# Sliding-window attention with a gated MLP: q loaded by 16 tokens per partition and turned straight through

## The chip, the cores and the metric

The kernel runs on one core of a Trainium2 chip. Its time is the device time of one launch in microseconds (us). The engines are named as in the profile: PE (TensorE, with PEld for its weight loads), DVE (VectorE), ACT (ScalarE), POOL (GpSimd) and SP (SyncE), which here only issues transfers. Sixteen DMA engines move the data between HBM and the on-chip memory SBUF.

## The reference

Eight batches, eight heads, 576 tokens, head size 64. Attention is causal in a window of 64 tokens; its output, with the heads side by side, goes through a gated MLP whose gate mixes the tokens with a 576 x 576 matrix.

```python
scores = scale * np.matmul(q, k.transpose(0, 1, 3, 2))     # scale = 1/8
mask = (rel >= 0) & (rel < 64)                             # rel = query token - key token
attn = softmax(np.where(mask, scores, -1e9))
x = matmul(attn, v), heads side by side                    # [8, 576, 512]
h = np.maximum(x @ w_in, 0.0);  u, v = h[..., :512], h[..., 512:]
v_n = (v - mean(v)) / sqrt(var(v) + 1e-6)
v_s = einsum('ts,bsd->btd', w_spatial, v_n) + b_spatial[None, :, None]
out = (u * v_s) @ w_out                                    # [8, 576, 512], float32
```

## The kernel before

The work is cut into named steps, and a table `ORDER` fixes by hand the order in which each engine's steps are issued, with the engine of the steps that may run on several. A step is named by its kind, its batch, and its part: `S4_1` are the score products of batch 4, head group 1. Engines run their steps in this order and wait for each other through semaphores. The SP queue (DQ in the table) issues all loads and nearly all stores, also in order; a store or a load whose buffer is not free holds up what is queued behind it.

A head group is four heads. For each batch and group, `load_steps` makes these steps for q, and the same for k:

- `ldq`: one transfer of the group's q, 4 heads x 576 tokens x 64 float32, into the tile `nq` of 128 partitions. Partition 32h + i holds 18 tokens in a row of head h, 18i to 18i + 17, a run of 4608 bytes.
- `cq`: a cast to float16, into `hq`, on POOL (three pieces), ACT or DVE as the table says.
- `tq`: one DVE transpose. Two float16 are taken as one float32, so a token is 32 such pairs. The instruction turns each 32 x 32 block by itself. Block j holds token 18i + j of all i, and it is written with a step of 18 pairs (72 bytes), so that in `qT` a partition holds one pair of head-size positions of one head, and the tokens stand in their order.

In `att_steps`, the step `S` computes the scores on PE. Each head has 32 partitions, and a product handles 64 keys and 64, 128 or 192 queries of one head. Each pair is two float16, so there are two products per block (w = 0 and 1), which read every second float16 of kT and qT, 4 bytes from token to token. A step has 64 products, into two PSUM pairs. There are 16 such steps, and in `rem_steps` a step `S_r` per batch with 32 products for the last 64 queries. ACT takes the exponentials (`E`, L477), DVE the mask (`M`, L480), PE the sums and the products with v (`Z`, `P`), ACT the inverse (`N`, `n`) and DVE the scaling (`X`, L512). The MLP follows with `V` and `U` (products with w_in), `A` (normalized), `G` (mixing over tokens) and `O` (w_out), its evacuations `Vr`, `Ur` and `Oe` on ACT and `Ge` on DVE, and the stores `st`. PE alternates between the attention of one batch and the MLP of the batches before it. Twenty-five steps `D` on zeros keep PE going in the first stage.

Tiles come from rings of buffers: eight for `nq`, `nk` and the weights' staging together, four for the cast `hq`/`hk`, six for `qT`/`kT`. v is loaded in pieces of 128 tokens, in runs of 256 bytes.

Of the kernel before, what the change touches and what calls it, by code (L numbers as in the profile page):

```python
# [169 lines left out]
class Plan:  # L170
# [3 lines left out]
    def add(self, name, engs, key, fn, deps=(), acq=(), uses=(), mode=None, nbytes=0, n=0):  # L174
        if isinstance(engs, tuple):
            engs = [engs]
        s = Step(name, engs, key, fn, deps, acq, uses, mode, nbytes, n)
        s.n = len(self.steps)
        self.steps.append(s)
        return s  # L180
# [17 lines left out]
def kernel(  # L198
# [11 lines left out]
    nc = tc.nc  # L210
    f16 = dt.float16
    f32 = dt.float32
# [67 lines left out]
    def buf(tag, name):  # L280
        b = Buf(tag, name)
        if tag in SHAPES:
            shape, d = SHAPES[tag]
            b.make = lambda i: pool.tile(shape, d, tag=f"{tag}_{i}", bufs=1, name=name)
        return b

    plan = Plan()
    add = plan.add
    ENG = {"ACT": nc.scalar, "DVE": nc.vector, "POOL": nc.gpsimd, "PE": nc.tensor, "DQ": nc.sync}

    def cp(e, o, i):
        if e == "ACT":
            nc.scalar.copy(o, i)  # L293
        elif e == "POOL" and len(i.shape) == 2 and i.shape[1] > 1000:
            for n in (0, 384, 768):
                nc.gpsimd.tensor_copy(o[:, n:n + 384], i[:, n:n + 384])  # L296
        elif e == "POOL" and len(i.shape) == 4 and i.shape[1] > 2:
            for lo, hi in ((0, 2), (2, i.shape[1])):
                nc.gpsimd.tensor_copy(o[:, lo:hi, :, :], i[:, lo:hi, :, :])
        else:  # L300
            ENG[e].tensor_copy(o, i)

    def cost(n, a=True, d=True, p=True, d1=False):

        out = []
        if a:
            out.append(("ACT", 0.09 + 0.00083 * n))
        if d:
            out.append(("DVE", 0.07 + (0.00104 if d1 else 0.00053) * n))
        if p:  # L310
            out.append(("POOL", 0.14 + 0.00083 * n))
        return out
# [81 lines left out]
    KT, QT, HV, HS, DKT, DQT, DHV, XB, XD = {}, {}, {}, {}, {}, {}, {}, {}, {}  # L394

    def load_steps(b, g, key):
        early = b < 2

        def one(name, src, key):
            n = buf("nat", f"n{name}{b}_{g}")  # L400
            ld = add(f"ld{name}{b}_{g}", ("DQ", 0.45), key, lambda e: nc.sync.dma_start(
                n.t[:, :], src[b, 4 * g:4 * g + 4, :, :].rearrange("h (i j) d -> (h i) (j d)", j=18)),
                acq=[n], nbytes=1.57, n=128)
            h = buf("hqk", f"h{name}{b}_{g}")
            c = add(f"c{name}{b}_{g}", cost(1152, d=early), key,
                    lambda e: cp(e, h.t[:, :], n.t[:, :]), deps=[ld], acq=[h], uses=[n])
            qt = buf("qkT", f"{name}T{b}_{g}")
            d = add(f"t{name}{b}_{g}", ("DVE", 1.09), key, lambda e: nc.vector.transpose(  # L408
                qt.t[:, :].rearrange("p (i j) -> p j i", j=18),
                h.t[:, :].bitcast(f32).rearrange("p (j w) -> p j w", w=32)),  # L410
                deps=[c], acq=[qt], uses=[h])
            return qt, d

        KT[b, g], DKT[b, g] = one("k", k, key)
        QT[b, g], DQT[b, g] = one("q", q, key + 0.001)
        nv = buf("natv", f"nv{b}_{g}")
        lds = []
        for c in range(5):
            sn = 128 if c < 4 else 64
            lds.append(add(f"ldv{b}_{g}{c}", ("DQ", 0.42),  # L420
                           key + 0.002 + 0.0001 * c,
                           lambda e, c=c, sn=sn: nc.sync.dma_start(  # L422
                               nv.t[0:sn, c, :, :],
                               v[b, 4 * g:4 * g + 4, 128 * c:128 * c + sn, :].transpose([1, 0, 2])),
                           deps=lds[-1:], acq=[] if c else [nv], uses=[nv] if c else [],
                           nbytes=0.0051 * sn, n=4 * sn))
        hv = buf("hv", f"hv{b}_{g}")
        hs = buf("hs", f"hs{b}_{g}")
        parts = [(0, 2), (2, 4)] if early else [(0, 4)]
        done = []  # L430
        for n, (lo, hi) in enumerate(parts):
            w = hi - lo
            l0 = max(lo, 1)
            c = add(f"cv{b}_{g}{n}", cost(256 * w, d=early), key + 0.003,
                    lambda e, lo=lo, hi=hi: cp(e, hv.t[:, lo:hi, :, :], nv.t[:, lo:hi, :, :]),
                    deps=[lds[hi - 1]] + done[:1], acq=[hv] if n == 0 else [],
                    uses=[nv] + ([hv] if n else []))
            sl = add(f"sl{b}_{g}{n}", cost(256 * (hi - l0), d=early), key + 0.0035,
                     lambda e, l0=l0, hi=hi: cp(e, hs.t[0:64, l0:hi, :, :], hv.t[0:64, l0:hi, :, :]),
                     deps=[c] + done[1:2], acq=[hs] if n == 0 else [],  # L440
                     uses=[hv] + ([hs] if n else []))
            su = add(f"su{b}_{g}{n}", cost(256 * w, d=early), key + 0.0035,
                     lambda e, lo=lo, hi=hi: cp(e, hs.t[64:128, lo + 1:hi + 1, :, :],
                                                hv.t[64:128, lo:hi, :, :]),
                     deps=[c, sl if n == 0 else done[1]], uses=[hv, hs])
            done += [c, sl, su]
        done.append(add(f"s4{b}_{g}", cost(256, d=early), key + 0.004, lambda e: cp(
            e, hs.t[0:64, 4, :, :], nv.t[0:64, 4, :, :]), deps=[lds[4], done[1]], uses=[nv, hs]))
        HV[b, g], HS[b, g] = hv, hs
        DHV[b, g] = done  # L450

    def pair16(t):
        return t[:, :].bitcast(f16).rearrange("p (t w) -> p t w", w=2)

    def att_steps(b, g, key):
        sc = [buf("pair", f"sc{b}_{g}{u}") for u in (0, 1)]
        e2 = [buf("e2", f"e2_{b}_{g}{u}") for u in (0, 1)]

        def emit_S(e):
            kT, qT = pair16(KT[b, g].t), pair16(QT[b, g].t)  # L460
            with nc.named_scope(f"S{b}_{g}"):
                for m in range(4):
                    for w in (0, 1):
                        for kap in (2 * m, 2 * m + 1):
                            r = 64 * (kap % 2)
                            c0 = 0 if kap == 1 else 64 * kap
                            c1 = min(512, 64 * kap + 128)
                            for hh in range(4):
                                d = slice(32 * hh, 32 * hh + 32)
                                nc.tensor.matmul(sc[hh // 2].t[r:r + 64, hh % 2, c0:c1],  # L470
                                                 kT[d, 64 * kap:64 * kap + 64, w], qT[d, c0:c1, w],
                                                 start=(w == 0), stop=(w == 1))
        s = add(f"S{b}_{g}", ("PE", 0.6), key, emit_S, deps=[DKT[b, g], DQT[b, g]],
                acq=sc, uses=[KT[b, g], QT[b, g]], mode="s")
# [11 lines left out]
        for u in (0, 1):  # L486
# [3 lines left out]
            def emit_Z(e, u=u, zb=zb):  # L490
                with nc.named_scope(f"Z{b}_{g}{u}"):
# [4 lines left out]
                    acq=[zb], uses=[e2[u]], mode="v")  # L496
            lzd = inverse_steps(f"{b}_{g}{u}", zb, lz, z, key + 0.03 + 0.02 * u, 512)

            def emit_P(e, u=u, ob=ob):
                with nc.named_scope(f"P{b}_{g}{u}"):  # L500
# [7 lines left out]
            p = add(f"P{b}_{g}{u}", ("PE", 0.24), key + 0.04 + 0.02 * u, emit_P,  # L508
                    deps=[mins[u]] + DHV[b, g], acq=[ob], uses=[e2[u], hv, hs], mode="v")
# [17 lines left out]
    def rem_steps(b, key):  # L527
        sc = [buf("pair", f"scr{b}_{u}") for u in (0, 1)]

        def emit_S(e):  # L530
            with nc.named_scope(f"S{b}_r"):
                for g in (0, 1):
                    kT, qT = pair16(KT[b, g].t), pair16(QT[b, g].t)
                    for w in (0, 1):
                        for kap in (8, 7):
                            r = 64 * (kap % 2)
                            for hh in range(4):
                                d = slice(32 * hh, 32 * hh + 32)
                                nc.tensor.matmul(
                                    sc[hh // 2].t[r:r + 64, hh % 2, 64 * g:64 * g + 64],  # L540
                                    kT[d, 64 * kap:64 * kap + 64, w], qT[d, 512:576, w],
                                    start=(w == 0), stop=(w == 1))
        e2 = buf("er", f"er_{b}")
        s = add(f"S{b}_r", ("PE", 0.16), key, emit_S,
# [25 lines left out]
        def emit_P(e):  # L570
            with nc.named_scope(f"P{b}_r"):
# [9 lines left out]
        p = add(f"P{b}_r", ("PE", 0.14), key + 0.04, emit_P, deps=[mn] + DHV[b, 0] + DHV[b, 1],  # L581
                acq=[ob], uses=[e2, HS[b, 0], HS[b, 1]], mode="v")
# [213 lines left out]
    for b in range(B):  # L796
        for g in (0, 1):
            load_steps(b, g, (-1.0 + 0.1 * g) if b == 0 else b - 1.5 + 0.4 * g)
            att_steps(b, g, b + 0.36 * g)
        rem_steps(b, b + 0.72)  # L800
        gmlp_steps(b, b + 1.0)
# [40 lines left out]
```

## Time and profile before

| what | value |
|---|---|
| time, median of 3 runs | 203.01 us (202.39 to 203.58) |
| span of the profiled execution, first to last instruction | 201.0 us |
| mean granted PE clock | 0.996 |
| PE / DVE / ACT / POOL busy | 94% / 80% / 83% / 38% |
| share of DMA engine time in packets of the SP queue | 70.1% |
| DVE transposes of q, of k (16 each) | 1243 ns, 1247 ns |
| loads of q, of k (16 each), issue to landing | 6.4 us, 5.5 us |
| score steps S0_0 and S7_1 begin at | 8.67 us, 158.35 us |

No separate time of the profiled execution is given beside its span; the median of the runs is 2.0 us above the span. In the profile, DMA is the mean busy share of the sixteen DMA engines. Packets are the single runs that a DMA engine moves. In the groups of instructions, a line gives busy time and the mean of one instruction, then the idle time of the engine just before them and who ended it.

### The profile page before, as it was taken

What the parts mean: (1) busy time and instruction counts of PE and PEld (TensorE: products, weight loads), DVE (VectorE), ACT (ScalarE), POOL (GpSimd) and SP (SyncE); (2) the same over time, 40 slices, a digit from 0 to 9 for tenths busy, and PEclk for the clock granted to TensorE, in tenths of its full rate; (3) what the DMA queues carried; (4) which work ended last, traced back from release to release, by engine and by line L of the source; (5) the groups of instructions that cost most, each with busy time, mean ns of one, the idle gap of its engine ahead of it and who ended that gap; (6) DMA issues with size and microseconds to landing.
All of it is one profiled execution on the core that took longest, in us unless ns stands there. A gap on an engine that the chain in (4) does not pass through costs nothing.

```text
span 201.0 us, 7008 instructions
## 1 busy us (share of the span) xinstructions
PE 188.6 (94%) x2927; PEld 97.7 (49%) x2927; DVE 161.2 (80%) x307; ACT 167.0 (83%) x307; POOL 76.5 (38%) x144
## 2 busy tenths in 40 slices
PE   7588889899999999989999999999999999999992
PEld 2233535545445445654455545554465455444450
DVE  4699979999998999699699898979957796647430
ACT  2588799878999899897998989999999999457431
POOL 5202575675894398153757999000000000000000
PEclk9999999999999999999999999999999999999998
DMA  6997999899898876999859995897633004200345
GB/s 221 387 276 184 336 378 210 292 372 377 185 274 255 246 221 188 295 243 234 311 118 262 241 316 178 227 284 249 185 111 117 3 5 132 108 0 0 128 145 202
DMA packets 50275, 42.69 MB, mean 212 GB/s; under 512 B 39361, under 2 KB 39489, under 8 KB 50242
## 3 DMA queue, kind: packets, MB, share of 16 engines
q1 hardware_dynamic: 50018, 41.91, 70.1%
q8 instruction: 23, 0.38, 0.8%
q10 hardware_dynamic: 224, 0.33, 0.5%
q14 instruction: 10, 0.08, 0.1%
HBM read 32.79 MB, written 9.44 MB: 210 GB/s over the span
## 4 chain that ended last, share of the span: by engine, by line
PE 70%; DMA 9%; SPq 7%; ACT 5%; DVE 5%; POOL 1%; issue 1%; POOLq 0%
PE bank L738 16%; PE bank L653 12%; PE bank L763 12%; PE bank L708 10%; DMA nk<-in_k_dram 9%; SPq L422 4%; PE pair L470 4%; PE bank L504 3%; PE bank L666 3%; PE bank L493 3%; PE bank L744 2%; SPq L327 2%; ACT e L477 1%; PE bank L713 1%; ACT ob L610 1%
## 5 line engine op out<-in xcount | busy, mean ns | idle before, releaser
L738 PE MATMUL bank<-wspT,vn 128*128 128x512 f16 (+1 forms) x160 | 37.5, 379 | 0.0
L477 ACT ACTIVATE e<-pair 128x1024 f16<-128x1024 f32 x32 | 31.9, 1027 | 2.7 <-PE pair L470 2.5
L752 DVE TENSOR_TENSOR g<-bank,ru 128x512 f16<-128x512 f32 (+1 forms) x40 | 24.8, 632 | 11.0 <-PE bank L738 5.0
L708 PE MATMUL bank<-x,win 128*128 128x512 f16 x128 | 31.6, 379 | 0.0
L763 PE MATMUL bank<-wout,g 128*128 128x512 f16 x128 | 31.3, 379 | 0.0
L653 PE MATMUL bank<-win,x 128*128 128x512 f16 x128 | 30.4, 379 | 0.2 <-DVE x L512 0.2
L721 ACT ACTIVATE ru<-bank 128x512 f32<-128x512 f32 (+1 forms) x40 | 21.4, 562 | 8.4 <-PE bank L708 4.6
L635 DVE BATCH_NORM_STATS2 st<-vs 128x6 f32<-128x512 f16 (+1 forms) x40 | 25.9, 670 | 3.0 <-ACT vs L633 2.8
L512 DVE TENSOR_TENSOR x<-bank,lz 128x512 f16<-128x512 f32 x32 | 21.2, 683 | 5.4 <-PE bank L504 2.6
L633 ACT ACTIVATE vs<-bank 128x512 f16<-128x512 f32 (+1 forms) x40 | 22.9, 597 | 3.1 <-PE bank L653 2.3
L610 ACT COPY ob<-bank 128x512 f32<-128x512 f32 (+1 forms) x39 | 22.6, 588 | 3.3 <-PE bank L763 3.1
L738 PEld LDWEIGHTS <-vn 128*128 128x128 f16 (+1 forms) x160 | 14.9, 97 | 17.7 <-DVE vn L692 0.5
L480 DVE TENSOR_TENSOR e<-e,mask 128x1024 f16<-128x1024 f16 x32 | 22.5, 721 | 1.0 <-ACT e L477 1.0
L408 DVE STREAM_TRANSPOSE qT<-hq 128x576 f32<-128x576 f32 x16 | 19.7, 1243 | 2.5 <-POOL hq L296 2.3
L296 POOL CAST hq<-nq 128x384 f16<-128x384 f32 x33 | 16.5, 536 | 13.1 <-DMA nq<-in_q_dram 12.5
L408 DVE STREAM_TRANSPOSE kT<-hk 128x576 f32<-128x576 f32 x16 | 20.0, 1247 | 1.4 <-ACT hk L293 1.1
L519 ACT ACTIVATE lz<-bank 128x512 f32<-128x512 f32 x32 | 18.6, 603 | 2.1 <-PE bank L493 2.0
L521 ACT ACTIVATE lz<-lz 128x512 f32<-128x512 f32 x32 | 19.6, 631 | 0.1
L653 PEld LDWEIGHTS <-x 128*128 128x128 f16 x128 | 12.0, 97 | 14.3 <-issue 0.6
L708 PEld LDWEIGHTS <-win 128*128 128x128 f16 x128 | 11.9, 98 | 14.4 <-issue 1.3
L763 PEld LDWEIGHTS <-g 128*128 128x128 f16 x128 | 11.8, 98 | 13.4 <-issue 0.5
L692 DVE TENSOR_SCALAR vn<-vs,mv,ln 128x512 f16<-128x512 f16 (+1 forms) x40 | 15.4, 436 | 3.5 <-ACT ln L682 3.3
(85 smaller groups left out, 294.7 us busy)
## 6 DMA issues: line engine op xcount, KB each, us to landing
nq<-in_q_dram SPq DMA_DIRECT2D x16, 576.0 KB, 6.4
nk<-in_k_dram SPq DMA_DIRECT2D x16, 576.0 KB, 5.5
nv<-in_v_dram SPq DMA_DIRECT2D x64, 128.0 KB, 4.9
out_dram<-ob SPq DMA_DIRECT2D x14, 512.0 KB, 4.6
wi<-in_moe_w_in_dram SPq DMA_DIRECT2D x8, 256.0 KB, 5.6
ws<-in_moe_w_spatial_dram SPq DMA_DIRECT2D x4, 288.0 KB, 8.2
nv<-in_v_dram SPq DMA_DIRECT2D x16, 64.0 KB, 3.6
wo<-in_moe_w_out_dram SPq DMA_DIRECT2D x4, 256.0 KB, 7.1
```

Source lines behind the costliest of these rows:

```text
L408: d = add(f"t{name}{b}_{g}", ("DVE", 1.09), key, lambda e: nc.vector.transpose(qt.t[:, :].rearrange("p (i j) -> p j i", j=18), h.t[:, :].b ...
L477: ex = add(f"E{b}_{g}{u}", ("ACT", 0.91), key, lambda e, u=u: nc.scalar.activation(e2[u].t[:, :, :], sc[u].t[:, :, :], AF.Exp, bias=0.0, s ...
L480: mins.append(add(f"M{b}_{g}{u}", ("DVE", 0.65), key, lambda e, u=u: nc.vector.tensor_tensor(e2[u].t[:, :, :], e2[u].t[:, :, :], mask[:, : ...
L610: lambda e: (nc.vector.tensor_copy if last else nc.scalar.copy)(view(), m.t[rows, 0:n]),
L633: rl = add(f"Vr{b}_{j}", ("ACT", 0.49), key, lambda e: nc.scalar.activation(vs.t[0:jn, :], m.t[0:jn, :], AF.Relu), deps=[pv], acq=[vs], us ...
L635: s1 = add(f"Vb{b}_{j}", ("DVE", 0.6), key + 0.02, lambda e: nc.vector.bn_stats(st6.t[0:jn, 0:6], vs.t[0:jn, :]), deps=[rl], acq=[st6], us ...
L653: nc.tensor.matmul(m.t[:, :], xr(b, r)[:, 128 * j:128 * j + 128], w_in_sb[r][:, 512:1024], start=(r == 0), stop=(r == 3))
L708: nc.tensor.matmul(m.t[:, :], w_in_sb[r][:, 128 * i:128 * i + 128], xr(b, r), start=(r == 0), stop=(r == 3))
L721: lambda e, m=m, ru=ru, n=n: nc.scalar.activation(ru.t[:, 0:n], m.t[:, 0:n], AF.Relu), deps=[pu], acq=[ru], uses=[m])))
L738: nc.tensor.matmul(m.t[:, :], w[0:kn, 128 * i:128 * i + 128], wspT[kk][0:kn, 0:512], start=(kk == 0), stop=(kk == 4))
L752: lambda e, m=m, g=g, ru=ru, n=n: nc.vector.tensor_tensor(g.t[:, 0:n], m.t[:, 0:n], ru.t[:, 0:n], ALU.mult),
L763: nc.tensor.matmul(m.t[:, :], G[r][0].t[:, 128 * j:128 * j + 128], w_out_sb[r][:, :], start=(r == 0), stop=(r == 3))
```

## The change

q is loaded in two transfers. The first brings tokens 0 to 511, 16 tokens per partition (runs of 4096 bytes), the second tokens 512 to 575, two per partition (runs of 512 bytes), both into the same tile. k is loaded as before. The DVE transpose of q then writes its blocks straight through: token 16i + j stands in column 32j + i of `qT`, and token 512 + 2i + j in column 512 + 32j + i. The score products get their queries in the order of tokens by reading q's columns with two steps: 16 (or 2) columns that are 32 pairs (128 bytes) apart, and then on by one pair (4 bytes). The queue table, the casts and the rest are the same.

```diff
+            def load(e):
+                if name == "k":
+                    nc.sync.dma_start(n.t[:, :], src[b, 4 * g:4 * g + 4, :, :].rearrange(
+                        "h (i j) d -> (h i) (j d)", j=18))
+                    return
+                for lo, hi, j in ((0, 512, 16), (512, 576, 2)):
+                    nc.sync.dma_start(n.t[:, 2 * lo:2 * hi], src[b, 4 * g:4 * g + 4, lo:hi, :].rearrange(
+                        "h (i j) d -> h i (j d)", j=j))
...
             d = add(f"t{name}{b}_{g}", ("DVE", 1.09), key, lambda e: nc.vector.transpose(
+                qt.t[:, :], h.t[:, :].bitcast(f32)) if name == "q" else nc.vector.transpose(
                 qt.t[:, :].rearrange("p (i j) -> p j i", j=18),
                 h.t[:, :].bitcast(f32).rearrange("p (j w) -> p j w", w=32)),
...
+    def toks(t, d, lo, hi, w):
+        v16 = t[:, :].bitcast(f16).rearrange("p (t w) -> p t w", w=2)
+        if lo < 512:
+            return v16[d, 0:512, w].rearrange("p (j i) -> p i j", i=32)[:, lo // 16:hi // 16, :]
+        return v16[d, 512:576, w].rearrange("p (j i) -> p i j", i=32)
...
-                                                 kT[d, 64 * kap:64 * kap + 64, w], qT[d, c0:c1, w],
+                                                 kT[d, 64 * kap:64 * kap + 64, w], toks(qT, d, c0, c1, w),
...
-                                    kT[d, 64 * kap:64 * kap + 64, w], qT[d, 512:576, w],
+                                    kT[d, 64 * kap:64 * kap + 64, w], toks(qT, d, 512, 576, w),
```

## The prediction

> **What bounds the kernel now.** I read the page's first two parts, then the chain that ended last, then the windows, then the rows of the lines that the diff touches.
>
> ```profile
> span 201.0 us, 7008 instructions
> PE 188.6 (94%) x2927; PEld 97.7 (49%) x2927; DVE 161.2 (80%) x307; ACT 167.0 (83%) x307; POOL 76.5 (38%) x144
> DMA  6997999899898876999859995897633004200345
> GB/s 221 387 276 184 336 378 210 292 372 377 185 274 255 246 221 188 295 243 234 311 118 262 241 316 178 227 284 249 185 111 117 3 5 132 108 0 0 128 145 202
> DMA packets 50275, 42.69 MB, mean 212 GB/s; under 512 B 39361, under 2 KB 39489, under 8 KB 50242
> PE 70%; DMA 9%; SPq 7%; ACT 5%; DVE 5%; POOL 1%; issue 1%; POOLq 0%
> ```
>
> PE is busy for 94% of the span and carries 70% of the chain: this is a PE-bound kernel after its first 40 us. But the second resource is close behind. The windows (DMA share is the mean busy share of the 16 DMA engines, the last two columns are share and GB/s):
>
> ```profile
> 40.00:50.00 10.00, 9.82 (x160) 5.37 (x160) 9.42 (x14) 7.99 (x14) 6.42 (x13) 1.00 1.06 373
> 0.00:147.00 147.00, 138.61 (x2317) 71.73 (x2318) 130.30 (x245) 129.86 (x239) 76.51 (x144) 1.00 0.89 258
> 147.00:201.00 54.00, 50.01 (x612) 26.00 (x610) 30.86 (x62) 37.15 (x70) 0.00 (x0) 0.98 0.25 88
> ```
>
> Up to 147 us, when the last q load has landed (it is issued at 141.0), the DMA engines are 89% busy: 0.89 x 147 = 131 us on each of the sixteen. They have 16 us of slack there, no more. A full DMA engine moves 373 / 16 = 23.3 GB/s.
>
> The rows of the lines that change (mean ns of one before the second bar):
>
> ```profile
> L408 DVE STREAM_TRANSPOSE qT<-hq 128x576 f32<-128x576 f32 x16 | 19.7, 1243 | 2.5 <-POOL hq L296 2.3
> L470 PE MATMUL pair<-qT,kT 32*64 32x128 f16 x768 | 12.2, 225 | 4.3 <-DVE kT L408 2.6 <-DVE qT L408 1.7
> L512 DVE TENSOR_TENSOR x<-bank,lz 128x512 f16<-128x512 f32 x32 | 21.2, 683 | 5.4 <-PE bank L504 2.6 <-PE bank L738 1.8 <-ACT hs L293 0.6
> L583 DVE TENSOR_TENSOR x<-bank,lz_r 128x256 f16<-128x256 f32 x8 | 3.4, 421 | 3.1 <-PE bank L575 2.7 <-ACT lz_r L521 0.4
> nq<-in_q_dram SPq DMA_DIRECT2D x16, 576.0 KB, 6.4
> ```
>
> **Part 1, the q loads: the part that I think decides.** Before, a q load is 128 runs of 4608 B at one equal step: one list of 128. After, the first transfer is 4 heads x 32 runs of 4096 B. Head to head is 36,864 elements, 32 runs are 32,768, so the two levels do not fuse and the outermost level of the source has 4 entries. The second is 4 x 32 runs of 512 B. How far such a transfer is spread over the sixteen DMA engines is not shown by any row of before, so it is bounded from both sides: all sixteen (no cost) or four, one for each head.
>
> The page has a hint. v is read in 16 x (4 x 512 + 256) = 36,864 runs of 256 B. The rest of the 39,361 packets under 512 B is 2,497 = 16 x 156 + 1. Part 6 of the page, with the one-run bias load wsb, lists 157 transfers. I read this as one small completion packet from each engine that took part: sixteen for each of the 156 transfers with 64 or 128 runs outermost, one for wsb, whose pattern has one. So the spread follows the shape. I take four engines.
>
> The Trainium skill, "DMA: Bandwidth & Descriptors", section "Why a DMA increments its semaphore by 16 and not by 1", says that the engine count is the largest number up to 16 that divides the slowest dimension above one of both sides' patterns. By that rule 4 and 128 give four engines, always the lowest-numbered four; the packet count of before agrees for 156 + 1 transfers, and none there has a 4 outermost.
>
> The cost: a q load is 589,824 B. Over sixteen engines that is 36,864 B each, 1.58 us at 23.3 GB/s; over four it is 147,456 B, 6.33 us. Each of the four carries 4.75 us more per load, 76 us over 16 loads, on top of 131: 207 us of work before the last q is there. At 24.2 GB/s (the slice with 387) and with the 131 cut by the 1.06 that full windows read, it is 124 + 73 = 197, less the v pieces and stores behind that load (about 5 us): 192. I take 200. The other twelve idle more, which helps nobody, since all later loads still need all sixteen.
>
> Does SP keep the four fed? Its queue is in order and waits for copies in front of stores. But each store stands behind later loads than its copy needs: st2_4 (issued at 107.0) has thirteen q loads ahead of it, and Oe2_4, for which it waits, follows S4_r and needs ten of them. Three loads, 19 us of the four engines' work, lie between. So I count no gap, and 5 us in the upper end.
>
> After the last landing: 2 us for landing (the first q load, issued at 0.81, is there at 4.84, of which 1.6 is moving), cast 1.16 (ACT L293), turn 0.75 to 1.24, then S7_1. In before S7_1 begins at 158.35 and the end is at 201.0: 42.65 us of work which follows it in PE's written order. So 200 + 2 + 2.1 + 42.65 = 246.8.
>
> **Part 2, the q turns.** Sixteen of 1243 ns, with writes 72 B apart. What a straight write costs, no row shows. The nearest rows are L512 against L583: (683 - 421) / 256 = 1.02 ns an element, 0.16 fixed, so 576 elements 0.75 us. Bounds: 0.75 and 1.24 (no gain). I take 0.75: 16 x 0.49 = 7.9 us less DVE, on PE's path only in the first 40 us (DVE busy there 9.87 of 10 us from 10 to 20, 9.94 from 30 to 40; three or four turns, 1.5 to 2 us). Under part 1 that is hidden behind the loads except for the last turn, which is in the sum.
>
> **Part 3, the score products.** 1024 + 256 matmuls read q with neighbours 128 B apart instead of 4. A step of 64 takes 0.70 us of PE (S7_1: 158.42 to 159.12 on the chain), a remainder step 0.26. The row for N = 128 (225 ns) lies on the contiguous ones, so 4 B costs nothing; 128 B is in no row. Bounds: no change; or the factor by which the turn with far-apart writes stands above the straight estimate, 1243 / 750 = 1.7, up to 4 if each column pays for itself. I take 2: +0.70 for each of 16 steps, +0.26 for each of 8, 13.3 us of PE in all. PE has 47 us more room under part 1, so only S7_1 and S7_r, in the tail, count: +0.96. At 4 it would be +2.9 there.
>
> The Trainium skill, "SBUF — State Buffer", section "Door 1: The DMA port swizzle", says that SBUF lines are 16 B and that each access crossing into a new line pays. By that rule the turns of q gain and the products lose; the 1243 ns of the 72 B writes agree, no row shows the reading side, and the sum by it is the same 13.3 us, without a price of its own.
>
> **Part 4, issues.** 16 more DMA issues on SP at 476 ns (median of L401 for nq), 7.6 us, behind which k, v and weight loads stand. While the DMA engines are full SP waits for them anyway (six v issues take 8.55 us from 4.63 on), so I count nothing under part 1; with its cover gone three of them come ahead of k1_1, which is on the chain: +1.4. Casts are the same instructions, now waiting for two transfers.
>
> Sum: 246.8 + 1.0 = 247.8 span. The profiled execution has a span of 201.0 against a median of 203.01 of the three runs, 2.0 outside. **249.8 us.** Ends of this case: 192 + 2 + 1.9 + 42.65 + 2 = 240; 207 + 5 + 2 + 2.4 + 42.65 + 2.9 + 2 = 264.
>
> **Rivals.** *A. The q loads spread over sixteen engines after all, and the products read at full pace: not slower.* The place is DVE in the first 40 us; the gain is 1.5 to 2 us, less up to 1.4 for the issues. For it: DVE is full there and S1_1 waits for a q turn on the chain (28.92, 1.27 us). Against: a nested source and the packet count above; far-apart reading must be free while far-apart writing seems not to be. It decides as soon as q loads land within the present 6.4 us. Time 201.5, from 200 to 204. If the turn gains nothing either, the change is only split loads: 203 to 204.
>
> *B. Spread over sixteen, but the products pay.* PE is the bound then and nothing covers it: 13.3 us less the 2 of part 2, 214; from 208 (factor 1.7, partly hidden by the overlap of two neighbouring products) to 240 (factor 4). For it: PE 94%. Against: as A.
>
> **How the numbers follow.** Four engines 0.78; A 0.09; B 0.13. A measurement of this kernel tells about 0.5% (1 us) from no change. Faster: most of A, 0.06. Same: the rest, 0.03. Slower: 0.91. The range takes the first case whole and reaches down into B's likely part: 210 to 264; it leaves out A (0.09), the lowest part of B (0.02) and the tails of the first case (about 0.07).
>
> **What would show it.** Packets under 512 B: 39,361 - 256 + 128 = 39,233 with four engines, 39,617 with sixteen. The time to landing of nq above 12 us instead of 6.4. The DMA row near 6 in the first 200 us (the bytes are the same: mean about 172 GB/s) while casts and PE wait for nq. L408 for qT near 750 ns, kT at 1247. An S step near 1.4 us. Wrong would be: nq landing within 8 us (A or B; the S step then says which), or gaps in the DMA row with SP waiting for copies (above the range).

## The result

The changed kernel takes 279.83 us in the median of four runs (276.32 to 283.84, the profiled one 278.34), against 202.7 us before. Two of the four, and some executions of the kernel before, came out over 1.5% longer than the fastest of their kernel; among the others the changed kernel is slower by a factor of 1.373 (95% interval 1.356 to 1.391). The direction and the mechanism that the prediction put first are there; the time lies above the range (264 us).

The page of the changed kernel, its first two parts, the packets and the shares of the chain:

```profile
span 276.6 us, 7027 instructions
PE 225.1 (81%) x2927; PEld 113.8 (41%) x2927; DVE 157.0 (57%) x307; ACT 169.1 (61%) x307; POOL 75.0 (27%) x144
...
DMA  4626689685837636486654855549976450040044
GB/s 110 135 102 162 153 237 267 164 221 147 250 111 169 139 103 172 107 209 206 163 163 96 243 169 141 131 118 282 275 196 202 112 181 15 5 172 2 0 173 171
DMA packets 52195, 42.69 MB, mean 154 GB/s; under 512 B 39233, under 2 KB 41409, under 8 KB 52162
PE 32%; DMA 30%; SPq 22%; POOL 6%; ACT 6%; issue 2%; DVE 1%; POOLq 0%; ACTq 0%
```

PE has fallen from 94% to 81% and from 70% of the chain to 32%; DMA and the queue that issues it have taken over 52%. Yet the DMA row, the mean over sixteen engines, is lower than before, around 6 where it was 9: the kernel waits for DMA while over a third of the engines' time is idle (share 0.63 up to 222 us). The packets under 512 B are 39,233, the very number that the prediction gave for four engines (sixteen would have been 39,617).

The lines that answer to those of before: the turns, and the score products by shape.

```profile
L415 DVE STREAM_TRANSPOSE qT<-hq 128x576 f32<-128x576 f32 x16 | 12.3, 771 | 43.1 <-POOL hq L296 33.8
L416 DVE STREAM_TRANSPOSE kT<-hk 128x576 f32<-128x576 f32 x16 | 20.0, 1247 | 6.6 <-POOL hk L296 5.2
L484 PE MATMUL pair<-qT,kT 32*64 32x128 f16 x768 | 31.6, 395 | 17.7 <-DVE kT L416 9.7 <-DVE qT L415 8.0
L484 PE MATMUL pair<-qT,kT 32*64 32x192 f16 x128 | 13.8, 507 | 0.0
L484 PE MATMUL pair<-qT,kT 32*64 32x64 f16 x128 | 7.0, 290 | 0.0
```

The straight turn takes 771 ns instead of 1243, while k's, unchanged, stays at 1247. The products have gone from 225 to 395 ns at 128 columns. By the slope between 64 and 192 columns a column costs (507 - 290) / 128 = 1.70 ns.

The waits of the changed kernel, us in total, times, and the longest; the first of them was 12.5 us in before:

```profile
POOL hq L296 <- DMA nq<-in_q_dram: 72.1, 11, 11.9
DVE qT L415 <- POOL hq L296: 33.8, 8, 10.4
ACT hk L293 <- DMA nk<-in_k_dram: 18.7, 3, 12.9
```

And the chain, some of its pieces in order of time (start, us):

```profile
72.86 17.91 DMA nq<-in_q_dram
112.90 12.05 DMA nq<-in_q_dram
154.04 10.62 DMA out_dram<-ob
196.67 1.93 PE pair L484 x48
205.63 1.93 PE pair L484 x46
221.04 1.92 PE pair L484 x45
233.08 1.90 PE pair L484 x50
```

Up to S6_0 at 196.67 the chain goes through q loads that hold it for 10 to 18 us at a time, and also through a store that stands behind them for 10.62 us and so holds an output buffer that ACT waits for. From S6_0 on PE has little else to wait for: 79.9 us to the end, where before it was 201.0 - 125.8 = 75.2. The 4.7 us more there are about what the four score steps cost, 1.2 us more each. The other 70.9 us come before S6_0.

### The profile page after: what moved, and what is told of

Read it like the earlier page. It is cut to its first block, busy times and chain, and to the rows that moved or that the text cites. A ratio compares the mean times of both kernels' runs of the same rounds, so it can differ in the third digit from the quotient of the medians.

```text
span 276.6 us, 7027 instructions
## 1 busy us (share of the span) xinstructions
PE 225.1 (81%) x2927; PEld 113.8 (41%) x2927; DVE 157.0 (57%) x307; ACT 169.1 (61%) x307; POOL 75.0 (27%) x144
## 2 busy tenths in 40 slices
DMA packets 52195, 42.69 MB, mean 154 GB/s; under 512 B 39233, under 2 KB 41409, under 8 KB 52162
## 4 chain that ended last, share of the span: by engine, by line
PE 32%; DMA 30%; SPq 22%; POOL 6%; ACT 6%; issue 2%; DVE 1%; POOLq 0%; ACTq 0%
DMA nq<-in_q_dram 24%; SPq L430 13%; PE bank L752 8%; SPq L408 7%; PE bank L777 6%; PE bank L722 4%; DMA out_dram<-ob 4%; PE bank L667 4%; PE pair L484 3%; DMA nk<-in_k_dram 2%; POOL hs L299 2%; POOL hk L296 2%; POOL hq L296 1%; PE bank L507 1%; POOL hv L299 1%
## 5 line engine op out<-in xcount | busy, mean ns | idle before, releaser
L484 PE MATMUL pair<-qT,kT 32*64 32x128 f16 (+2 forms) x1024 | 31.8, 396 | 17.7 <-DVE kT L416 9.7
L752 PE MATMUL bank<-wspT,vn 128*128 128x512 f16 (+1 forms) x160 | 40.3, 397 | 2.5 <-DVE vn L706 2.5
L722 PE MATMUL bank<-x,win 128*128 128x512 f16 x128 | 34.4, 405 | 5.4 <-ACT vs L647 5.4
L777 PE MATMUL bank<-wout,g 128*128 128x512 f16 x128 | 32.6, 390 | 5.7 <-ACT ru L735 4.0
L415 DVE STREAM_TRANSPOSE qT<-hq 128x576 f32<-128x576 f32 x16 | 12.3, 771 | 43.1 <-POOL hq L296 33.8
L667 PE MATMUL bank<-win,x 128*128 128x512 f16 x128 | 32.7, 399 | 3.1 <-ACT lz_r L533 3.1
L296 POOL CAST hq<-nq 128x384 f16<-128x384 f32 x33 | 15.5, 505 | 72.1 <-DMA nq<-in_q_dram 72.1
L484 PEld LDWEIGHTS <-kT 32*64 32x64 f16 x1024 | 22.4, 124 | 26.2 <-DVE kT L416 10.2
L706 DVE TENSOR_SCALAR vn<-vs,mv,ln 128x512 f16<-128x512 f16 (+1 forms) x40 | 17.3, 483 | 7.3 <-ACT ln L696 7.3
```

Of the source, the lines that this page charges most:

```text
L484: nc.tensor.matmul(sc[hh // 2].t[r:r + 64, hh % 2, c0:c1], kT[d, 64 * kap:64 * kap + 64, w], toks(qT, d, c0, c1, w), start=(w == 0), stop= ...
L667: nc.tensor.matmul(m.t[:, :], xr(b, r)[:, 128 * j:128 * j + 128], w_in_sb[r][:, 512:1024], start=(r == 0), stop=(r == 3))
L722: nc.tensor.matmul(m.t[:, :], w_in_sb[r][:, 128 * i:128 * i + 128], xr(b, r), start=(r == 0), stop=(r == 3))
L752: nc.tensor.matmul(m.t[:, :], w[0:kn, 128 * i:128 * i + 128], wspT[kk][0:kn, 0:512], start=(kk == 0), stop=(kk == 4))
L777: nc.tensor.matmul(m.t[:, :], G[r][0].t[:, 128 * j:128 * j + 128], w_out_sb[r][:, :], start=(r == 0), stop=(r == 3))
```

## The experiments

Three theories. Theory 1: the outermost level of 4 runs puts a q load on four DMA engines, and they set the pace. Theory 2: the slow score reads set the time. Theory 3: more and smaller transfers per load do.

**Loads alone.** The loads of the changed kernel, with the turn and the reads of before.

```diff
-                qt.t[:, :], h.t[:, :].bitcast(f32)) if name == "q" else nc.vector.transpose(
-                                                 kT[d, 64 * kap:64 * kap + 64, w], toks(qT, d, c0, c1, w),
+                                                 kT[d, 64 * kap:64 * kap + 64, w], pair16(qT)[d, c0:c1, w],
...
```

> q loaded in the two transfers of the changed kernel, turn and reads as before; the tokens' order in q is not undone, so scores belong to other tokens; the work is the same. Theory 1: the loads' pace stays, and only the score steps of the last PE-bound 80 us give back 4 x 1.2 us, less what the slower turns take: 265 to 275 us. Theory 2: 203 us. Theory 3: 265 to 278 us, as theory 1.

Measured: 278.22 us, 1.375 (1.356 to 1.394) of before. The loads by themselves bring the whole loss; theory 2 is out as the cause of the time. The give-back of some 5 us did not show. With the short score steps PE is not the bound after S6_0 either: the chain goes on through the last loads, with pieces such as these (start, us):

```profile
202.34 11.57 DMA nq<-in_q_dram
218.57 8.54 DMA nv<-in_v_dram
235.03 0.69 PE pair L483 x53
```

S7_1 begins at 235.03, 2 us later than in the changed kernel, and 42.8 us remain after it (42.65 in before).

**Turn and reads alone.** The load of before, the rest as changed.

```diff
-                for lo, hi, j in ((0, 512, 16), (512, 576, 2)):
-                    nc.sync.dma_start(n.t[:, 2 * lo:2 * hi], src[b, 4 * g:4 * g + 4, lo:hi, :].rearrange(
-                        "h (i j) d -> h i (j d)", j=j))
+                nc.sync.dma_start(n.t[:, :], src[b, 4 * g:4 * g + 4, :, :].rearrange(
+                    "h (i j) d -> (h i) (j d)", j=18))
```

> q loaded as before (one transfer of 18 tokens per partition), turn and reads as in the changed kernel; the queries stand in another order than the reads take them for, so scores belong to other tokens; the work is the same. Theory 1: 203 + 20.4 - 2 = 221 us, nq lands in about 6.4 us. Theory 2: 278 us. Theory 3: 203 us or less.

Measured: 219.31 us, 1.084 (1.074 to 1.094). This is what the reads cost without the cover of the loads: 17 us. The two costs do not add: 278 is not 278 + 17, since PE has time while it waits for q.

**Four engines with nothing else.** The kernel before, but a q load takes every second head, so that its four heads do not fuse into one list. One transfer, runs of 4608 B as ever.

```diff
-                n.t[:, :], src[b, 4 * g:4 * g + 4, :, :].rearrange("h (i j) d -> (h i) (j d)", j=18)),
+                n.t[:, :], src[b, g:8:2, :, :].rearrange("h (i j) d -> h i (j d)", j=18)),
```

> The kernel before with one thing changed: a q load, still one transfer of 18 tokens per partition in runs of 4608 B, takes every second head (heads g, g+2, g+4, g+6), so that its source is 4 x 32 runs that do not fuse; the heads of q and k then do not belong together, the work is the same. Theory 1 (four engines): as the loads of the changed kernel alone, 265 to 285 us, completion packets 16 x 12 fewer (39,169 under 512 B). Theory 3 (two transfers, runs of 4096 and 512 B): 203 us. If 4096-byte runs on equal boundaries are what makes the packets slow, 245 to 255 us, as the prediction's price has it.

Measured: 277.15 and 283.87 us; the profile is of the first. The page of this kernel:

```profile
span 275.4 us, 7008 instructions
DMA packets 50083, 42.69 MB, mean 155 GB/s; under 512 B 39169, under 2 KB 39297, under 8 KB 50050
```

The packets of 512 B and over are those of before; only the completion packets are 192 fewer, 12 for each q load. Neither a second transfer nor the 4096-byte runs are needed for the loss. Theory 3 is out, and so is the thought that runs on equal boundaries make the packets slow.

**The same transfers on sixteen engines.** Runs of 4096 and 512 B in two transfers, laid at 18 tokens per partition, so that 128 runs stand outermost.

```diff
-                for lo, hi, j in ((0, 512, 16), (512, 576, 2)):
-                    nc.sync.dma_start(n.t[:, 2 * lo:2 * hi], src[b, 4 * g:4 * g + 4, lo:hi, :].rearrange(
-                        "h (i j) d -> h i (j d)", j=j))
+                for lo, hi in ((0, 1024), (1024, 1152)):
+                    nc.sync.dma_start(n.t[:, lo:hi], src[b, 4 * g:4 * g + 4, :, :].rearrange(
+                        "h (i j) d -> (h i) (j d)", j=18)[:, lo:hi])
```

> The changed kernel with the same two transfers (128 runs of 4096 B, 128 of 512 B) but laid at 18 tokens per partition, so that 128 runs stand outermost; turn and reads as in the changed kernel, scores belong to other tokens. Theory 1: 219 us as with the load before, 39,361 + 16 x 16 = 39,617 small packets. Theory 3: 260 to 278 us, as the transfers and packets are those of the changed kernel.

Measured: 222.88 us, 1.100 (1.091 to 1.108), 39,617 small packets. Against the single transfer with the same turn and reads (219.31) the second transfer costs about 3.6 us, though the intervals of the two ratios just overlap; whether the 16 more issues or the small runs carry it was not separated.

**Two engines.** Each transfer of a q load cut into two of two heads.

```diff
-                    nc.sync.dma_start(n.t[:, 2 * lo:2 * hi], src[b, 4 * g:4 * g + 4, lo:hi, :].rearrange(
-                        "h (i j) d -> h i (j d)", j=j))
+                    for h2 in (0, 2):
+                        nc.sync.dma_start(n.t[32 * h2:32 * h2 + 64, 2 * lo:2 * hi], src[
+                            b, 4 * g + h2:4 * g + h2 + 2, lo:hi, :].rearrange("h (i j) d -> h i (j d)", j=j))
```

> As the changed kernel, but each of the two transfers of a q load is cut into two of two heads, so that the outermost level is 2. Theory 1: two engines carry all of q, 15.8 us per load on each instead of 7.9, 16 x 7.9 = 126 us more on the two; by the sixth batch 14 loads, 110 us: about 385 us, between 350 and 410. Theory 2: 278 us. Theory 3: 16 x 2 transfers more: 278 to 300 us.

Measured: 371.25 us in one run. S6_0 begins at 278.0, 152 us later than in before; with four engines it was 70.9 us later. Fourteen q loads stand ahead of its k load in the queue: 10.9 us a load on two engines, 5.1 us on four. The delay goes with the load that one engine carries.

**Head by head.** Eight transfers of 32 runs for each q load.

```diff
-                    nc.sync.dma_start(n.t[:, 2 * lo:2 * hi], src[b, 4 * g:4 * g + 4, lo:hi, :].rearrange(
-                        "h (i j) d -> h i (j d)", j=j))
+                    for h4 in range(4):
+                        nc.sync.dma_start(n.t[32 * h4:32 * h4 + 32, 2 * lo:2 * hi], src[b, 4 * g + h4, lo:hi, :].rearrange(
+                            "(i j) d -> i (j d)", j=j))
```

> q loaded head by head: each transfer has 32 runs outermost, eight transfers per q load instead of two; turns and reads as in the changed kernel. Theory 1 (a transfer whose outermost level is 4 runs on four engines, and that sets the pace): the loads come back to sixteen engines; packets under 512 B rise to 39,361 - 256 + 16 x 8 x 16 = 41,153; what is left is the slower score step (1.92 us instead of 0.70, 16 x 1.2 + 8 x 0.15 = 20.4 us of PE) less about 2 us for the turns: 221 us, up to 235 if 112 more issues hold SP up. Theory 2 (the slow score reads alone set the time): 278 us. Theory 3 (more transfers and packets per load cost the time): above 278 us.

Measured: 238.74 us, 1.180 (1.166 to 1.194), 41,153 small packets. It takes back some 40 us, as theory 1 has it, but stands 19.4 us above the kernel with the load of before and above its own expectation. It has 112 more issues on SP, and its runs of 4096 B took 240 ns on the mean in the packet records of its trace, against 200 in the kernel with the same transfers on sixteen engines and 159 for an undisturbed one (the 5th percentile of either). Which of the two carries the 19 us was not separated.

**The turn alone.** Load and reads as before, only the straight turn.

```diff
+                qt.t[:, :], h.t[:, :].bitcast(f32)) if name == "q" else nc.vector.transpose(
...
-            kT, qT = pair16(KT[b, g].t), pair16(QT[b, g].t)
+            kT, qT = pair16(KT[b, g].t), QT[b, g].t
...
-                                                 kT[d, 64 * kap:64 * kap + 64, w], qT[d, c0:c1, w],
+                                                 kT[d, 64 * kap:64 * kap + 64, w], pair16(qT)[d, c0:c1, w],
...
```

> The kernel before with the straight q turn alone (load and reads as before, so that scores belong to other tokens). If the turns' 16 x 0.47 us reach the end only in the DVE-bound first 40 us: 1 to 2 us faster, 201 us. If DVE is off the path there too: no difference, within 1 us. If DVE limits later stages as well: up to 7.5 us faster.

Measured: 1.000 of before (0.996 to 1.004). 7.6 us less DVE work (761 ns a turn instead of 1243) changes nothing that can be measured; the first guess was wrong.

**How the reads pay.** First the two steps of the read exchanged: eight neighbouring columns, then 128 B on.

```diff
-            return v16[d, 0:512, w].rearrange("p (j i) -> p i j", i=32)[:, lo // 16:hi // 16, :]
+            return v16[d, 0:512, w].rearrange("p (j i) -> p j i", i=32)[:, :, lo // 16:hi // 16]
```

> Load as before, turn straight, and the reads with their two steps exchanged: 8 (or 32) neighbouring columns 4 B apart, then 128 B on; the scores stand in another order. If a column that is far from its neighbour costs, the score step falls from 1.92 us back to 0.70 to 0.85 us and the time to 201 to 203 us. If a pattern with two steps costs, it stays at 1.92 us and 219 us.

Measured: 0.996 of before (0.992 to 1.001), a step takes 0.70 us. The pattern with two steps is free; far-apart neighbours are not. Then one step of 8 bytes through all of qT, and of 16 bytes with `s=4` in place of `s=2`:

```diff
-        if lo < 512:
-            return v16[d, 0:512, w].rearrange("p (j i) -> p i j", i=32)[:, lo // 16:hi // 16, :]
-        return v16[d, 512:576, w].rearrange("p (j i) -> p i j", i=32)
+        v = t[:, :].bitcast(f16).rearrange("p (t w) -> p t w", w=2)[d, 0:512, w].rearrange("p (c s) -> p s c", s=2)
+        if hi - lo == 192:
+            return v[:, 0:2, 0:96]
+        return v[:, 0, 0:hi - lo]
```

> Load before, straight turn, one-step reads of every second column of qT (8 B apart; the scores belong to other tokens). If the cost begins where neighbours no longer share 16 bytes: 0.70 us per score step, 202 us. If it grows with the distance from 4 B on: about 1.0 us, 207 us.

> The same with every fourth column (16 B apart). If each column then comes from a line of its own and that is the cost: 1.9 us per score step, 219 us, as with 128 B. If the distance of 128 B is what costs: between 0.7 and 1.3 us.

Measured: 204.86 and 220.28 us, one run each; a score step takes 1.05 and 1.95 us. Groups by shape, first of the kernel with runs of eight, then with 8 B, then with 16 B:

```profile
L483 PE MATMUL pair<-qT,kT 32*64 32x128 f16 x768 | 12.3, 224 | 2.6 <-DVE kT L415 1.4 <-DVE qT L414 1.2
L483 PE MATMUL pair<-qT,kT 32*64 32x192 f16 x128 | 6.0, 260 | 0.0
L483 PE MATMUL pair<-qT,kT 32*64 32x64 f16 x128 | 4.8, 205 | 0.0
```

```profile
L483 PE MATMUL pair<-qT,kT 32*64 32x128 f16 x768 | 18.0, 290 | 3.4 <-DVE kT L415 3.0 <-DVE qT L414 0.4
L483 PE MATMUL pair<-qT,kT 32*64 32x192 f16 x128 | 8.3, 341 | 0.0
L483 PE MATMUL pair<-qT,kT 32*64 32x64 f16 x128 | 4.9, 234 | 0.0
```

```profile
L483 PE MATMUL pair<-qT,kT 32*64 32x128 f16 x768 | 32.6, 403 | 2.2 <-DVE kT L415 2.2
L483 PE MATMUL pair<-qT,kT 32*64 32x192 f16 x128 | 13.7, 508 | 0.0
L483 PE MATMUL pair<-qT,kT 32*64 32x64 f16 x128 | 6.8, 290 | 0.0
```

By the slope between 64 and 192 columns a column costs 0.43 ns with runs of eight, 0.84 at 8 B, 1.70 at 16 B, and 1.70 at 128 B. It doubles with the distance up to 16 B and then stays. The expectation that 8 B would be free was wrong.

Last, the results written to PSUM 64 B apart, which puts the queries of the runs of eight back in order:

```diff
-                                nc.tensor.matmul(sc[hh // 2].t[r:r + 64, hh % 2, c0:c1],
+                                nc.tensor.matmul(sc[hh // 2].t[r:r + 64, hh % 2, c0:c1].rearrange("p (i j) -> p j i", j=16),
...
```

> As the kernel with the exchanged steps (load before, straight turn, runs of 8 neighbouring columns), and the products write their results to PSUM with two steps (64 B from column to column, then 4 B on), which restores the order that the reads gave up. If far-apart writes to PSUM are free: score step 0.70 to 0.85 us, 202 us. If each far-apart result pays as a far-apart read does: 1.9 us, 219 us.

Measured: 204.67 us, 1.015 (1.003 to 1.027); a score step takes 1.01 us, 304 ns at 128 columns. Far-apart writes pay, but less than far-apart reads. With the turn alone worth nothing, none of these points to a version faster than before.

## Why the prediction was wrong

**Right.** Four engines: 39,233 packets, and the kernel with nothing but the four-run source has the whole loss. The turn: 0.75 us forecast, 0.77 measured. The tail: S7_1 to the end forecast at 42.65 + 0.96 = 43.6 us, measured 276.6 - 233.08 = 43.5, in part by luck: the score step there costs 1.2 us more where 0.70 was taken. That the reads cost nothing on the path before the tail: loads alone take as long as all of it.

**The term that failed** is the work of the four engines before the last q: "I take 200", from 6.33 us a load on each. S7_1 was to begin at 204 and began at 233; these 29 us are the miss (278.34 - 249.8 = 28.5). By the packet records of the trace (size and duration of every packet) the last q packet ended at 223.4 us; the sum had it there at 202. That is 21 of the 29 us. The price came from a window in which all sixteen engines run alike. Two windows of the changed kernel show what it left out, and one of before stands beside them (last two columns: DMA share, GB/s):

```profile
5.00:9.00 4.00, 2.77 (x8) 0.83 (x6) 0.00 (x0) 0.00 (x0) 0.00 (x0) 1.00 1.04 206
16.00:20.00 4.00, 2.50 (x66) 1.84 (x67) 2.52 (x2) 1.77 (x3) 0.00 (x0) 0.50 0.26 98
```

```profile
3.00:7.00 4.00, 3.62 (x13) 1.30 (x11) 1.55 (x8) 0.87 (x1) 1.61 (x4) 1.00 1.01 395
```

From 16 to 20 us four engines of sixteen are busy (0.26) and move 98 GB/s, 24.5 each: the full rate that was taken. From 5 to 9 us the four carry q while k runs on the others; all sixteen are busy and together move 206 GB/s, half of the 395 that they move in before. In that stretch the lopsided load slows its own packets and those beside it: a q run of 4096 B takes 360 ns there (171 from 16 to 20 us), a k run of 4608 B 363 ns (187 for the runs of that size in the window of before). Why, on the memory's side or the receiving one, no run here settles.

Over the whole trace the effect is smaller. A q run of 4096 B takes 215 ns on the mean and one of 512 B 31 ns; 32 of each come to 7.9 us of packet time a load on each of the four, 126 us over 16 loads where the forecast had 101. But the same runs on sixteen engines took 200 and 28 ns, which is 7.3 us for 32 of each, and in before 32 of the runs of 4608 B came to 7.0 us (219 ns each). So about half of what the price lacked (6.33, or 6.7 in packet time, since its window read 1.06) was in the mean packet times of ordinary traffic, which the full window did not show; the rest came with the lopsided load.

With all other traffic taken as spread evenly, each of the four had 237 us of packet time up to 223.4 us, a share of 1.06, which is what full windows read; the forecast had 207, or 212 with its price for q in packet time. So on the mean the four were full all that time, and the sum of their work was mis-sized by 25 to 30 us, most of it q. The granted PE clock fell too (0.89 up to 222 us, 1.00 after), but with the four engines full all that time it is not needed to explain the delay.

The prediction counted on the engines' idle time being eaten, and it was: up to S6_0 an engine had 114 us of packet time in 126 us in before (0.91), each of the four 207 in 197 in the changed kernel (1.06). S6_0 came 70.9 us late behind fourteen loads, 5.1 us each.

The other 8 us of the 29 lie behind the last q packet: S7_1 began 9.7 us after it, where about 2 were counted. In the changed kernel PE, the bound from S6_0 on, was not yet at S7_1; in the kernel with the loads alone the chain goes through the last q loads and a v load behind them, and S7_1 began at 235.0. The two bounds lie within 2 us. "No gap" was wrong too: SP waited 7.2 us in front of the last q load with a store (released, by the profile's inference, by ACT at L694), and no q packet moved from 210.9 to 215.8 us. The prediction had 5 us for this in its upper end.

**Part 3** was undersized: 2 was taken as the factor of a score step, 1.92 / 0.70 = 2.7 was measured. As the bound it would have come to 17 us net (the run with turn and reads alone), where rival B gave 214, 11 us above before. **Part 2**'s 1.5 to 2 us of gain do not exist. Rival A is ruled out.

The Trainium skill, "DMA: Bandwidth & Descriptors", section "Why a DMA increments its semaphore by 16 and not by 1", gives four engines here and two for the cut transfers: the packet counts and the two delays, 5.1 and 10.9 us a load, agree. The Trainium skill, "SBUF — State Buffer", section "Door 1: The DMA port swizzle", says that two hits in a 16-byte line are enough for full bandwidth. The measured reads differ: at two columns per line a column costs 0.84 ns instead of 0.43, and the measurement decides. That each access in a new line pays, as it also says, agrees: the cost no longer grows past 16 B.

## What to carry to other kernels

Look at the outermost level of both sides of a transfer after fusing, before looking at its bytes: a split that keeps four heads apart from their rows turns a sixteen-engine load into a four-engine one, and the DMA row then looks idle while the kernel waits for DMA. A quarter of the engines can cost somewhat more than four times the even share: 7.9 us of packet time a load on each engine here, against 1.8 for the same runs on sixteen. Price such a load by the mean packet time of the kernel's own traffic, and not by a window at full rate. A layout that saves time on an engine with slack is paid wherever its columns are read: keep at least four neighbouring float32-sized columns together in a matmul's moving operand.

## What the runs showed of the hardware that was not expected

All sixteen DMA engines can read as fully busy at half the bytes (share 1.04 at 206 GB/s, against 1.01 at 395). A score product's columns cost 0.43, 0.84, 1.70 and 1.70 ns at 4, 8, 16 and 128 bytes from column to column, as if each 16-byte stretch that is touched cost 1.7 ns in these steps. PSUM results 64 bytes apart make a score step 1.01 us instead of 0.70.
